# Attention in front of two expert layers: the second batch's v loads issued by GpSimd, raw weights issued two steps sooner, the decoder's VectorE part behind the normalisation

## The chip, the cores and the metric

The kernel runs on one core of one Trainium2 chip. The metric is the device time of one execution in microseconds (us), and the figure that stands for a kernel is the median of its timed runs. A profile is one more execution, recorded by the hardware profiler; its span runs from the first to the last instruction. The engines are called PE (TensorE, matrix products), DVE (VectorE), ACT (ScalarE), POOL (GpSimd) and SP (SyncE, which only issues transfers here).

## The reference, cut to what matters

```python
# q, k, v: (2 batches, 8 heads, 576 rows, 64), float32
scores = scale * np.matmul(q, k.transpose(0, 1, 3, 2))
mask_plain = (rel >= 0) & (rel < 32)                      # heads 0 to 3
mask_dil = (rel >= 0) & (rel < 128) & (rel % 4 == 0)      # heads 4 to 7
scores = np.where(masks, scores, -1e9)
attn = softmax(scores)                                    # with + 1e-9 in the sum
x = np.matmul(attn, v)                                    # then (2 * 576, 512)
...
h = x @ w_in                                              # first layer, 512 -> 2048 -> 512
g = h * np.tanh(softplus(h))
x = g @ w_out
...
for e in range(4):                                        # second layer, 4 experts
    out += p[:, e:e+1] * (np.maximum(x @ w1[e], 0.0) @ w2[e])
```

The weights `w_in` and `w_out` arrive as 64-bit floats, 8 bytes for each value.

## The kernel before

Attention is cut into ten units, `au[0]` to `au[9]`: five chunks of up to 128 rows (`c` = 0 to 4, the last one of 64 rows) in each of two batches. Every unit passes the same stations: its k and q are loaded (`load_k`, `load_q`, four buffers each), transposed by PE, spread by ACT into `kk` and `qq` (`spread`), multiplied (`scores`, one PSUM bank), put through `softmax` (DVE twice, ACT once), transposed again (`probsT` on PE, `probsT_copy` on ACT), multiplied with v (`values`, PSUM bank 4), divided by the row sums (`sums`, `normalise`, both DVE), transposed (`xT`) and split into a high and a low part (`x_hi` on ACT, `x_lo` on DVE) in `xh` and `xl`, which the first layer reads.

A window of keys reaches back 32 rows (or 32 rows of every fourth row), so v is kept in two tiles, `vP` (heads 0 to 3) and `vD` (heads 4 to 7), in which half of the partitions hold a chunk's own rows and the other half those before them. The own half is loaded from memory, as one list of transfers for each range of chunks (`v_loads`; eight transfers for two chunks, six for the last one, ten for chunks 2 to 4). The other half is copied from it by POOL, chunk by chunk (`copy_v(c)`), and `values` of a chunk needs both. One pair of tiles serves both batches: the loads of the second batch overwrite what the first batch has used.

The order on every engine is written out by hand: each engine runs its instructions in the order of the program text, and waits on semaphores where another engine's result is needed. A wait holds up all that stands behind it on that engine. A prologue handles units 0 to 4 as single calls, then `att_step(s)` runs for s = 3 to 7, with unit s at its scores, unit s-1 at its values, unit s-2 at its last transposition and unit s+2 at its first. So `values` of unit 4 is in step 5, of unit 5 in step 6, of unit 6 in step 7, and of units 7, 8 and 9 behind the steps. The copies of step s are those of unit s+1: chunk 4 of the first batch in step 3, chunks 0 to 3 of the second batch in steps 4 to 7.

All transfers are issued by SP. `load(jobs, *large)` deals a list of small v transfers out between large ones: the second batch's v come in three lists, ahead of step 3 with the k and q of unit 8, behind step 4 with two raw weight loads, and behind step 5 with one.

The raw weights are the 64-bit floats, loaded in halves of a unit of 512 KB (`dec_load`, four buffers), and decoded to 32 bits in pieces that lie between the attention's work from step 6 (`DEC0`) on: `dec_dve` (two DVE instructions, the first of which waits for the raw load, lines 151 and 158), then `dec_act` (ACT lines 168 and 175, POOL line 176), which also asks for the next raw load.

Behind the attention come the first layer (`Step1`, lines 570 and 592) and the second (lines 777 and 852), in which PE works without a break.

Of the kernel before, what the change touches and what calls it, by code (L numbers as in the profile page):

```python
# [23 lines left out]
def kernel(  # L24
# [13 lines left out]
    PE, ACT, DVE, POOL, SP = nc.tensor, nc.scalar, nc.vector, nc.gpsimd, nc.sync  # L38
# [70 lines left out]
    def unit_tiles(u):  # L109
        n = slice(1024 * u, 1024 * (u + 1))  # L110
        if u < NUA:
            units[u] = (wxh[:, n], wxl[:, n])
        elif u == NUA:
            units[u] = late[0:2]
        else:
            n = slice(1024 * (u - NUA - 1), 1024 * (u - NUA))
            units[u] = (late[2][:, n], late[3][:, n])
# [4 lines left out]
    def dec_load():  # L122


        if nld[0] >= len(halves) or not free_raws:
            return
        u, part = halves[nld[0]]
        nld[0] += 1
        t = free_raws.pop(0)
        dst = t[:, 1:4097]  # L130
        if part == 0:
            SP.dma_start(out=dst.rearrange("p (c f) -> p c f", c=4),
                         in_=w_in.bitcast(U8)[:, 1024 * u:1024 * (u + 1)].rearrange("(c p) f -> p c f", p=128))
        else:
            SP.dma_start(out=dst, in_=w_out.bitcast(U8)[128 * u:128 * (u + 1), :])
        staged[u, part] = t

    def half_at(n):
        return halves[n] if 0 <= n < len(halves) else None

    def part_cols(part):
        return slice(512 * part, 512 * part + 512)

    def dec_dve():


        n = ndec[0]
        h = half_at(n)
        if h:

            DVE.tensor_scalar(out=kwbuf[n % 3], in0=staged[h].bitcast(U32)[:, 2:1026:2], scalar1=24, scalar2=None,
                              op0=ALU.logical_shift_left)
        h = half_at(n - 1)
        if h:

            kw = kwbuf[(n - 1) % 3]
            t = staged.pop(h)
            DVE.scalar_tensor_tensor(out=kw, in0=t.bitcast(U32)[:, 1:1025:2], scalar=5, in1=kw,
                                     op0=ALU.logical_shift_right, op1=ALU.bitwise_or)
            free_raws.append(t)  # L160

    def dec_act():
        n = ndec[0]
        h = half_at(n)
        if h:

            kw = kwbuf[n % 3]
            ACT.activation(kw.bitcast(F16)[:, 1:1024:2], kw.bitcast(F32), AF.Copy)
        h = half_at(n - 1)
        if h:  # L170
            u, part = h
            if part == 0:
                unit_tiles(u)
            w, (hi, lo) = kwbuf[(n - 1) % 3].bitcast(F32), (t[:, part_cols(part)] for t in units[u])
            ACT.activation(hi, w, AF.Copy)
            POOL.tensor_tensor(out=lo, in0=w, in1=hi.bitcast(F32), op=ALU.subtract)
            dec_load()
        ndec[0] += 1
# [8 lines left out]
    NCH = (S + 127) // 128  # L187
# [61 lines left out]
    def keep():  # L249
        t = bank(7)  # L250
        for n in range(2):
            PE.matmul(t, warm[:, 0:128], warm, start=n == 0, stop=n == 1)
# [6 lines left out]
    def v_loads(b, c0, c1):  # L259

        g0, g1 = 4 * c0, min(4 * c1, S // 32)
        cf = min(c1, S // 128)
        jobs = []
        for j in range(2):
            own = slice(64 * j + 32, 64 * j + 64)
            for p in range(2):
                src = v[b, 2 * p + j:2 * p + j + 1]
                jobs.append((vP[own, p, g0:g1, j, :],
                             bass.AP(src.tensor, src.offset + 32 * g0 * D, [[D, 32], [32 * D, g1 - g0], [1, D]])))
            src = v[b, 4 + j:5 + j]  # L270
            for p in range(2 if cf > c0 else 0):
                jobs.append((vD[own, p, j, c0:cf, :],
                             bass.AP(src.tensor, src.offset + (2 * p * S + 128 * c0) * D,
                                     [[4 * D, 32], [128 * D, cf - c0], [1, 4 * D]])))
            if cf < c1:
                n = (S - 128 * cf) // 4
                jobs.append((vD[64 * j + 32:64 * j + 32 + n, :, j, cf, :],
                             bass.AP(src.tensor, src.offset + 128 * cf * D, [[4 * D, n], [2 * S * D, 2], [1, 4 * D]])))
        return jobs

    def load(jobs, *large):

        large = [w for w in large if w]
        step = -(-len(jobs) // len(large)) if large else len(jobs)
        for i in range(0, max(len(jobs), step), step):
            for o, x in jobs[i:i + step]:
                SP.dma_start(out=o, in_=x)
            if large:
                large.pop(0)()
        for w in large:  # L290
            w()

    def copy_v(c):

        g0, g1 = max(4 * c, 1), min(4 * c + 4, S // 32)
        for j in range(2):
            before, own = slice(64 * j, 64 * j + 32), slice(64 * j + 32, 64 * j + 64)
            POOL.tensor_copy(vP[before, :, g0:g1, j, :], vP[own, :, g0 - 1:g1 - 1, j, :])
            if c:
                POOL.tensor_copy(vD[before, :, j, c, :], vD[own, :, j, c - 1, :])  # L300
# [151 lines left out]
    au = [Unit(b, c) for b in range(B) for c in range(NCH)]  # L452
    NA = len(au)
    u0, u1, u2, u3, u4 = au[0:5]
    for u in (u0, u1, u2):
        u.load_k()
        u.load_q()
    first = v_loads(0, 0, 2)
    load(first[0:6], u3.load_k)
    load(first[6:8], u3.load_q)  # L460

    u0.transposes()
    u4.load_k()
    u4.load_q()
    copy_v(0)
    u0.spread()
    u1.transposes([0])
    u0.scores()
    u1.spread_k(range(2))
    u1.transposes([1])  # L470
    u1.spread_q()
    u0.softmax()
    u2.transposes()
    load(v_loads(0, 2, NCH)[0:8])
    load(v_loads(0, 2, NCH)[8:10], au[5].load_k, au[5].load_q)

    copy_v(1)
    zero_v(2)
# [33 lines left out]
    u0.x_lo()  # L512
    u2.probsT()
    u4.transposes()
    load(v_loads(1, 0, 2), au[8].load_k, au[8].load_q)

    def att_step(s):
        n2, n1, u, p1, p2 = (au[n] for n in (s + 2, s + 1, s, s - 1, s - 2))
        dec = s >= DEC0
        p1.probsT_copy()  # L520
        copy_v(n1.c)
        n1.spread()
        u.scores()
        u.softmax()
        if dec:
            dec_dve()
            keep()
        p1.sums()
        p1.values()
        p2.xT()  # L530
        p1.normalise()
        p2.x_hi()
        if dec:
            dec_act()
        p2.x_lo()
        n2.transposes()
        u.probsT()

        if s == 3:
            au[9].load_k()  # L540
            au[9].load_q()
        elif s == 4:
            load(v_loads(1, 2, 4), dec_load, dec_load)
        elif s == 5:
            load(v_loads(1, 4, NCH), dec_load)
        elif s == 6:
            dec_load()

# [58 lines left out]
    for n in (0, 1):  # L607
        o = 2 * GW * (n + 1)
# [285 lines left out]
    for s in range(3, NA - 2):  # L894
        att_step(s)
    SP.dma_start(out=prob, in_=probs.rearrange("(t p) e -> p t e", p=128))

    u3, u2, u1 = au[NA - 3:]
# [153 lines left out]
```

## Time and profile before

| | us |
|---|---|
| median of 3 timed runs | 649.11 |
| lowest and highest of them | 648.29, 3526.74 |
| the profiled execution's own time | 646.37 |
| its span | 644.5 |
| mean granted clock of PE in it | 0.993 |

The profiled execution took 1.9 us more than its span, and 2.7 us less than the median. Terms read from the span carry over to the median as differences.

### The profile page before, as it was taken

What the parts mean: (1) busy time and instruction counts of PE and PEld (TensorE: products, weight loads), DVE (VectorE), ACT (ScalarE), POOL (GpSimd) and SP (SyncE); (2) the same over time, 40 slices, a digit from 0 to 9 for tenths busy, and PEclk for the clock granted to TensorE, in tenths of its full rate; (3) what the DMA queues carried; (4) which work ended last, traced back from release to release, by engine and by line L of the source; (5) the groups of instructions that cost most, each with busy time, mean ns of one, the idle gap of its engine ahead of it and who ended that gap; (6) DMA issues with size and microseconds to landing.
All of it is one profiled execution on the core that took longest, in us unless ns stands there. A gap on an engine that the chain in (4) does not pass through costs nothing.

```text
span 644.5 us, 10164 instructions
## 1 busy us (share of the span) xinstructions
PE 629.7 (98%) x4156; PEld 561.5 (87%) x4158; DVE 287.8 (45%) x482; ACT 262.0 (41%) x497; POOL 179.1 (28%) x201
## 2 busy tenths in 40 slices
PE   8879999999999999999999999999999999999997
PEld 4757788889999999898989899898899998899986
DVE  5767777632211324454443522534522544523223
ACT  6666877643232344433244322344222334322220
POOL 8743455531200143152134300143300244200000
PEclk9998999999999999999999999999999999999999
DMA  9883576500000221210022300032200023000102
GB/s 187 171 215 110 187 228 208 187 0 1 1 1 1 65 66 66 66 66 3 0 66 99 98 1 1 1 98 84 81 1 0 22 81 95 2 2 14 52 1 81
DMA packets 51358, 43.66 MB, mean 68 GB/s; under 512 B 26352, under 2 KB 44144, under 8 KB 51312
## 3 DMA queue, kind: packets, MB, share of 16 engines
q1 hardware_dynamic: 51312, 43.02, 23.7%
q8 instruction: 32, 0.52, 0.3%
q14 instruction: 14, 0.11, 0.1%
HBM read 40.65 MB, written 2.36 MB: 67 GB/s over the span
## 4 chain that ended last, share of the span: by engine, by line
PE 92%; DMA 3%; ACT 2%; SPq 1%; issue 1%; DVE 1%; POOL 0%; DVEq 0%; POOLq 0%; ACTq 0%
PE bank L852 31%; PE bank L777 26%; PE bank L592 16%; PE bank L570 15%; DMA natq<-in_q_dram 2%; DMA vP<-in_v_dram 1%; SPq L322 1%; PE bank L405 1%; ACT late L619 1%; PE bank L335 1%; PE bank L438 1%; PE bank L417 1%; PE bank L375 1%; PE bank L421 1%; PE bank L383 0%
## 5 line engine op out<-in xcount | busy, mean ns | idle before, releaser
L777 PE MATMUL bank<-xh,late 128*128 128x256 f32 (+1 forms) x512 | 120.1, 295 | 2.6 <-ACT late L789 1.6
L777 PE MATMUL bank<-wxh,late 128*128 128x320 f32 (+1 forms) x384 | 94.0, 294 | 0.0
L777 PEld LDWEIGHTS bank<-xh,late 128*128 128x128 f32 x512 | 88.6, 188 | 5.6 <-ACT late L789 2.2
L852 PE MATMUL bank<-late,gh 128*128 128x512 f32 x288 | 89.3, 391 | 0.0
L570 PE MATMUL bank<-xh,late 128*128 128x320 f32 (+1 forms) x288 | 76.5, 337 | 0.0
L777 PE MATMUL bank<-xl,late 128*128 128x256 f32 (+1 forms) x256 | 75.3, 294 | 0.0
L592 PE MATMUL bank<-gh,late 128*128 128x320 f32 (+1 forms) x288 | 72.6, 337 | 0.0
L731 POOL TENSOR_TENSOR raw<-raw 128x256 f32<-128x256 f32 x16 | 12.2, 763 | 216.2 <-DVE late L620 210.3
L777 PEld LDWEIGHTS bank<-wxh,late 128*128 128x128 f32 x384 | 67.9, 188 | 0.6
L579 DVE TENSOR_TENSOR gl<-scr,gh 128x512 fp32r<-128x512 f32 (+1 forms) x32 | 24.4, 764 | 82.0 <-ACT gh L578 82.0
L852 PEld LDWEIGHTS bank<-late,gh 128*128 128x128 f32 x288 | 52.3, 188 | 9.6
L620 POOL TENSOR_TENSOR late<-raw,late 128x1024 fp32r<-128x1024 f32 x16 | 38.8, 2426 | 73.0 <-ACT late L619 73.0
L575 ACT ACTIVATE scr<-bank 128x320 f32<-128x320 f32 (+1 forms) x48 | 23.5, 490 | 85.7 <-PE bank L570 85.6
L852 PE MATMUL bank<-late,gl 128*128 128x512 f32 x144 | 56.7, 394 | 0.0
L777 PE MATMUL bank<-wxl,late 128*128 128x256 f32 (+1 forms) x192 | 56.6, 295 | 0.1
L570 PEld LDWEIGHTS bank<-xh,late 128*128 128x128 f32 x288 | 50.7, 188 | 4.3
L592 PEld LDWEIGHTS bank<-gh,late 128*128 128x128 f32 x288 | 50.1, 188 | 4.2
L619 ACT ACTIVATE late<-raw 128x512 fp32r<-128x512 f32 (+1 forms) x64 | 48.0, 781 | 12.7 <-PE bank L852 12.7
L852 PE MATMUL bank<-late,late 128*128 128x512 f32 (+1 forms) x219 | 52.8, 388 | 0.0
L777 PEld LDWEIGHTS bank<-xl,late 128*128 128x128 f32 x256 | 48.1, 188 | 1.9
L570 PE MATMUL bank<-xl,late 128*128 128x320 f32 (+1 forms) x144 | 48.6, 337 | 0.0
L592 PE MATMUL bank<-gl,late 128*128 128x320 f32 (+1 forms) x144 | 48.6, 337 | 0.0
(152 smaller groups left out, 1133.5 us busy)
## 6 DMA issues: line engine op xcount, KB each, us to landing
raw<-in_moe_w_dram SPq DMA_DIRECT2D x32, 512.0 KB, 3.5
raw<-in_moe_w_out_dram SPq DMA_DIRECT2D x15, 512.0 KB, 3.6
raw<-in_moe_w_in_dram SPq DMA_DIRECT2D x9, 512.0 KB, 4.1
scr<-in_moe_w_in_dram SPq DMA_DIRECT2D x7, 512.0 KB, 4.3
natk<-in_k_dram SPq DMA_DIRECT2D x8, 256.0 KB, 4.5
natq<-in_q_dram SPq DMA_DIRECT2D x8, 256.0 KB, 4.9
out_dram<-scr SPq DMA_DIRECT2D x8, 256.0 KB, 2.0
vD<-in_v_dram SPq DMA_DIRECT2D x16, 64.0 KB, 3.4
```

Of the source, the lines that this page charges most:

```text
L322: SP.dma_start(out=t[0:self.n], in_=src[self.b, :, rows, :].rearrange("h t d -> t h d"))
L335: PE.transpose(o, nat[0:n, 128 * a:128 * a + 128], ident[0:n, 0:n])
L375: PE.matmul(s[32 * g:32 * g + 32, 128 * p:128 * p + 128], qq[:, p, t:t + 32], kk[:, p, :, t + 96:t + 160], start=False, stop=True, skip_gr ...
L570: PE.matmul(h, a[:, c, :], x[:, c, :], start=c == 0 and k == 0, stop=c == 3 and k == 2)
L575: ACT.activation(self.hc[:, self.w * i:self.w * (i + 1)], h, AF.Mish)
L579: DVE.tensor_tensor(out=self.glo, in0=self.hc, in1=self.ghi.bitcast(F32), op=ALU.subtract)
L592: PE.matmul(yacc[self.grp][d], a[:, 512 + 128 * d:640 + 128 * d], x[:, g], start=u == UORD[self.grp][0] and k == 0, stop=u == UORD[self.gr ...
L619: ACT.activation(hi, src, AF.Copy)
L620: eng.tensor_tensor(out=lo, in0=src, in1=hi.bitcast(F32), op=ALU.subtract)
L731: POOL.tensor_tensor(out=a22, in0=a21, in1=a22, op=ALU.add)
L777: PE.matmul(out, w, x(k), start=first and k == 0 and i == 0, stop=k == 1 and i == 2, skip_group_check=not first)
L852: PE.matmul(acc, x[:, s], a[:, cols], start=self.p == 0 and f == 0 and i == 0, stop=self.p == NP2 - 1 and f == 1 and i == 2, skip_group_ch ...
```

## The change

The v loads of the second batch, three lists of 8, 8 and 6 transfers, are issued by POOL (`load_v`) at the same three places of the text, and no longer by SP. The first raw load moves from behind step 4 to a place ahead of step 3; the second and third stay behind steps 4 and 5 and the fourth behind step 6, now with no v transfers around them in SP's queue. In the prologue the first batch's v transfers of chunks 2 to 4 (`v1`) are issued sooner and between the k and q of units 4 and 5, and unit 5's k and q now stand ahead of the last five and the last three of them. In `att_step`, `dec_dve` stands behind `normalise` and `x_hi` and no longer ahead of `sums`. `load` takes transfers and calls in the order in which they are given.

```diff
--- before.py
+++ after.py
@@ -278,17 +278,16 @@
                              bass.AP(src.tensor, src.offset + 128 * cf * D, [[4 * D, n], [2 * S * D, 2], [1, 4 * D]])))
         return jobs
 
-    def load(jobs, *large):
-
-        large = [w for w in large if w]
-        step = -(-len(jobs) // len(large)) if large else len(jobs)
-        for i in range(0, max(len(jobs), step), step):
-            for o, x in jobs[i:i + step]:
-                SP.dma_start(out=o, in_=x)
-            if large:
-                large.pop(0)()
-        for w in large:
-            w()
+    def load(*jobs):
+        for job in jobs:
+            if callable(job):
+                job()
+            else:
+                SP.dma_start(out=job[0], in_=job[1])
+
+    def load_v(jobs):
+        for o, x in jobs:
+            POOL.dma_start(out=o, in_=x)
 
     def copy_v(c):
 
@@ -455,24 +454,21 @@
     for u in (u0, u1, u2):
         u.load_k()
         u.load_q()
-    first = v_loads(0, 0, 2)
-    load(first[0:6], u3.load_k)
-    load(first[6:8], u3.load_q)
+    v0, v1 = v_loads(0, 0, 2), v_loads(0, 2, NCH)
+    load(*v0[0:6], u3.load_k, *v0[6:8], u3.load_q, v1[0])
 
     u0.transposes()
-    u4.load_k()
-    u4.load_q()
+    load(u4.load_k, v1[1], u4.load_q, *v1[2:5])
     copy_v(0)
     u0.spread()
     u1.transposes([0])
     u0.scores()
     u1.spread_k(range(2))
     u1.transposes([1])
+    load(au[5].load_k, *v1[5:7], au[5].load_q, *v1[7:10])
     u1.spread_q()
     u0.softmax()
     u2.transposes()
-    load(v_loads(0, 2, NCH)[0:8])
-    load(v_loads(0, 2, NCH)[8:10], au[5].load_k, au[5].load_q)
 
     copy_v(1)
     zero_v(2)
@@ -512,7 +508,9 @@
     u0.x_lo()
     u2.probsT()
     u4.transposes()
-    load(v_loads(1, 0, 2), au[8].load_k, au[8].load_q)
+    vl = [v_loads(1, *c) for c in ((0, 2), (2, 4), (4, NCH))]
+    load(au[8].load_k, au[8].load_q, dec_load)
+    load_v(vl[0])
 
     def att_step(s):
         n2, n1, u, p1, p2 = (au[n] for n in (s + 2, s + 1, s, s - 1, s - 2))
@@ -523,7 +521,6 @@
         u.scores()
         u.softmax()
         if dec:
-            dec_dve()
             keep()
         p1.sums()
         p1.values()
@@ -531,6 +528,7 @@
         p1.normalise()
         p2.x_hi()
         if dec:
+            dec_dve()
             dec_act()
         p2.x_lo()
         n2.transposes()
@@ -540,9 +538,11 @@
             au[9].load_k()
             au[9].load_q()
         elif s == 4:
-            load(v_loads(1, 2, 4), dec_load, dec_load)
+            dec_load()
+            load_v(vl[1])
         elif s == 5:
-            load(v_loads(1, 4, NCH), dec_load)
+            dec_load()
+            load_v(vl[2])
         elif s == 6:
             dec_load()
```

## Rows read from the trace of the kernel before

**Rows 1.** Chain that ended last, by engine, of the whole span, from the page.

```profile
PE 92%; DMA 3%; ACT 2%; SPq 1%; issue 1%; DVE 1%; POOL 0%; DVEq 0%; POOLq 0%; ACTq 0%
```

**Rows 2.** Waits of PE behind the attention: waiter, releaser, us, times, longest.

```profile
PE bank L777 <- ACT late L789: 1.6, 3, 0.5
```

**Rows 3.** Stretches: busy us (and instructions) by engine, granted clock, DMA share, GB/s.

```profile
20.00:24.00 4.00, 3.01 (x75) 2.31 (x72) 2.97 (x6) 2.64 (x9) 3.86 (x8) 1.00 0.90 202
...
36.00:40.00 4.00, 3.84 (x62) 2.92 (x63) 1.38 (x2) 2.12 (x4) 1.83 (x4) 1.00 0.80 179
40.00:44.00 4.00, 1.21 (x33) 0.73 (x26) 1.60 (x5) 1.32 (x3) 1.17 (x2) 1.00 1.09 232
44.00:48.00 4.00, 3.37 (x45) 2.60 (x46) 3.93 (x8) 3.24 (x6) 2.33 (x4) 0.68 0.73 241
48.00:52.00 4.00, 4.00 (x53) 3.06 (x57) 2.12 (x5) 2.42 (x8) 3.06 (x5) 0.50 0.64 177
52.00:56.00 4.00, 4.00 (x41) 3.22 (x33) 3.79 (x9) 2.27 (x4) 0.78 (x2) 0.97 0.25 60
```

**Rows 4.** PE in order of time: start, us, line, tiles, count, [idle before].

```profile
21.80 0.62 PE L421 MATMUL bank<-vD,pT 128*32 128x128 f32 x16
...
24.26 0.63 PE L335 MATMUL bank<-ident,natk 128*128 128x128 f32 x4 [1.25 <-ACT xh L446]
25.28 0.63 PE L335 MATMUL bank<-ident,natq 128*128 128x128 f32 x4 [0.40 <-DMA natq<-in_q_dram]
...
31.69 0.50 PE L417 MATMUL bank<-vP,pT 128*32 128x128 f32 x6
...
36.53 0.64 PE L417 MATMUL bank<-vP,pT 128*32 128x128 f32 x16
...
40.81 0.39 PE L252 MATMUL bank<-warm 128*128 128x512 bf16 x1
44.63 0.65 PE L417 MATMUL bank<-vP,pT 128*32 128x128 f32 x16 [3.42 <-POOL vP L298]
...
51.17 1.08 PE L417 MATMUL bank<-vP,pT 128*32 128x128 f32 x16
...
57.48 0.29 PE L417 MATMUL bank<-vP,pT 128*32 128x128 f32 x2
```

**Rows 5.** DVE in order of time.

```profile
42.22 0.43 DVE L151 TENSOR_SCALAR scr<-raw 128x512 uint32<-128x512 uint32 x1 [4.68 <-DMA raw<-in_moe_w_in_dram]
...
43.79 0.69 DVE L429 TENSOR_TENSOR xn<-bank,sm 128x512 f32<-128x512 f32 x1
```

**Rows 6.** POOL in order of time.

```profile
26.64 0.52 POOL L203 MEMSET vD<- 64x512 f32 x1
27.21 0.39 POOL L298 COPY vP<-vP 32x256 f32<-32x256 f32 x1
...
28.55 0.61 POOL L300 COPY vD<-vD 32x512 f32<-32x512 f32 x1
31.09 0.50 POOL L298 COPY vP<-vP 32x384 f32<-32x384 f32 x1 [1.92 <-DMA vP<-in_v_dram]
...
42.81 0.61 POOL L298 COPY vP<-vP 32x512 f32<-32x512 f32 x1 [2.88 <-DMA vP<-in_v_dram]
```

**Rows 7.** SP's issues of v: ns of one, min/median/max; then us to landing.

```profile
L287 SPq DMA_DIRECT2D vP<-in_v_dram x16: 311/447/1658, 13.3 to 43.0; - x16
...
DMA to landing us min/median/max: 2.2/4.0/4.7
```

**Rows 8.** SP in order of time.

```profile
18.09 0.93 SPq L287 DMA_DIRECT2D vD<-in_v_dram x2
19.12 0.38 SPq L322 DMA_DIRECT2D natk<-in_k_dram  x1
...
36.10 1.56 SPq L132 DMA_DIRECT2D raw<-in_moe_w_in_dram  x1
```

**Rows 9.** Issues between 36 and 37 us: KB, us from issue to landing.

```profile
raw<-in_moe_w_in_dram SPq DMA_DIRECT2D x1, 512.0 KB, 6.0
```

## The prediction, made before the change was run

> **What bounds the kernel now.** I read the chain that ended last first: PE carries 92% of it [rows 1]. Then the waits of PE behind the attention: the longest entry is 1.6 us in all, the longest single wait 0.5 us [rows 2]. From there on PE has no gap that this change could fill, so what the change gives is what it moves the end of the attention, some 62 us into the span, and it reaches the total one for one. A measurement of this kernel can tell about 2% (13 us) from no change.
>
> Next the stretches of 4 us [rows 3]. Two stand out. Between 40 and 44 us PE is busy for 1.21 us of 4. Behind that the granted clock is 0.68, 0.50 and 0.97 of full speed (the 0.50 is 1.2 GHz, the lower of the two levels) while PE shows 3.37, 4.00 and 4.00 us of work. The time lost to the clock is 4 x (0.32 + 0.50 + 0.03) = 3.4 us. The smaller gap lies between 20 and 24 us.
>
> Then the engines in order of time, to find what opened the large gap. PE stops at 41.20 (40.81 + 0.39) and takes up `values` of unit 6 at 44.63, 3.42 us later [rows 4]. The trace names a POOL copy as releaser. I don't believe that entry: unit 6 is chunk 1, whose copies were done long before, and the copy that ran then is of a later chunk; in the two steps before, `values` started at 31.69 and 36.53 without such a wait. What did end just then is `normalise` of unit 5 on DVE, from 43.79 to 44.48 [rows 5], which reads the PSUM bank that these `values` write. It was late because DVE stood 4.68 us at line 151, `dec_dve` of step 6, waiting for the first raw load until 42.22 [rows 5]. SP issued that load at 36.10 [rows 8], and it landed 6.0 us after [rows 9]. So the head of the stall is one late transfer, and the fault is that `sums` and `normalise` stand behind it on DVE.
>
> POOL had a wait of its own at that time, 2.88 us until 42.81, for v transfers of chunk 2 [rows 6]. Its copies were then about 7 us ahead of their reader, `values` of unit 7 at 51.17 [rows 4].
>
> **The change, part by part.**
>
> *Raw loads sooner, `dec_dve` behind `normalise`.* One answer for both: the wait at line 151 goes. The first raw load stands behind unit 8's k and q, ahead of step 3, and SP issues it some 5 to 10 us sooner, as 22 v issues of 0.45 us leave its queue [rows 7]. Even with the 6.0 us to landing it is there before step 6 at 36 us. Should it be late, `normalise` no longer stands behind it; `x_lo` of unit s-2 and `dec_act` on ACT do. Taken alone, the gain is the 3.4 us of idle PE and the 3.4 us of slow clock behind it: 6.8 us. What is late next is the question of the POOL part. The new place costs `dec_act` a later start (it follows `values` now), and behind it on ACT stand the next `probsT_copy` and `spread`, which `values` and `scores` need some 4 us later; I cost it at nothing, at most 0.5 us a step for two steps.
>
> *First batch's v and unit 5's k and q in a new order.* PE waited 1.25 and 0.40 us for the transposes of unit 5, at 24.26 and 25.28 [rows 4]; its k was issued at 19.12 [rows 8]. The trace names an ACT operation for the longer wait, but the k transfer of 5.0 us landed then. The new order puts this k and q, 512 KB, ahead of the last v of chunks 2 to 4. At the 202 GB/s of that stretch [rows 3] these v come up to 2.6 us later. The last ones were issued at 18.09 and after [rows 8], and PE used them at 21.80 [rows 4] with little to spare. So the wait of 1.65 us turns into one of 0 to 2 us: worth 0 +- 1.7 us. POOL's copies of chunk 2 wait for some of these v too, which moves POOL by about 0.7 us.
>
> *The v loads on POOL.* This decides. POOL's queue ran without a break to 27.16 (26.64 + 0.52), and then took the copies of chunk 4, 27.21 to 29.16 [rows 6], which `values` of unit 4 needs at 31.69 [rows 4]. The spare time there is 2.5 us. Now eight issues stand ahead of these copies. Behind them stand the copies of chunk 0 (1.1 us), eight issues, the copies of chunk 1 (2.4 us), six issues, and the copies of chunk 2 (2.4 us; one copy is 0.50 to 0.61 us [rows 6]). All of it is in one queue, and the last item frees `values` of unit 7.
>
> No row shows an issue on POOL. From below: the same v transfers took SP 0.31 us at the least and 0.45 in the median [rows 7]; POOL could also hand one over in less, down to nothing. From above: POOL may be held until the data has landed, 4.0 us in the median [rows 7], if an issue there is not let go at once; the longest that SP was held is 1.66 us [rows 7]. I take 0.8 us, between SP's median and SP's longest and nearer to the first: the work is the same in kind, and POOL's own small copies of as many bytes take 0.6 us [rows 6], so I don't expect POOL to be quicker at it than SP.
>
> The Trainium skill, DMA: Bandwidth & Descriptors, "Latency and other measured facts", gives about 1 us to the first byte for transfers issued by GpSimd and about 0.6 us for those of SP. At 1 us for each issue the sum below would end some 4 us later, an estimate from that page; no run here shows it yet.
>
> The sum, with d for one issue. POOL is free at 27.2 + 0.7 = 27.9. The copies of chunk 4 end at 27.9 + 8d + 1.95 = 36.3 for d = 0.8, against 31.69 when PE wants them, and PE is there a little sooner now. So a new stall of about 5 us opens in front of `values` of unit 4, longer than the old one of 3.42, and I let it cost the same drop in clock, 3.4 us. PE's own line from there: from 31.69 to 41.20 was 9.5 us of work, and from 44.63 to 51.17 it was 6.54 with 2.9 lost to the clock (51.17 - 45.4 at half speed), 3.7 at full speed. `values` of unit 7 could start at 36.3 + 9.5 + 3.4 + 3.7 = 52.9. POOL's line: 27.9 + 22d + 1.95 + 1.1 + 2.4 + 2.4 = 35.75 + 22d = 53.35. The later of the two counts: 53.4 against 51.17, 2.2 us late. Before, the slow clock went on to about 52.3, which cost another 0.5 us; that is not paid again. The copies of chunks 3 and 4 follow on POOL at 55.8 and about 59, ahead of their readers (57.48 before [rows 4], plus 1.7). The sum is +1.7 us: the 6.8 us gained are spent, and a little more. From the profiled execution's 646.4 us that is 648.1; from the median of 649.1, which lies 2.7 us higher, it is 650.8, and I say 651.
>
> **The rivals.**
>
> *The issue is cheap* (d up to 0.4). The copies of chunk 4 end by 33, PE waits 1 to 2 us there, too short for what the 1.25 us gap did not do either (clock 1.00 in that stretch [rows 3]), POOL's line ends at 44.6, and `values` of unit 7 starts at about 33 + 9.5 + 3.7 = 46.2: 5 us sooner, with the clock 5.5. That gives 643 to 644. For it speaks that SP does the same in 0.31 to 0.45 us; against it, the copies' 0.6 us.
>
> *The issue is dear: slower than before.* One mechanism: POOL's queue, 22 issues long, holds `values` of unit 7. From d = 1.3 on, POOL's line ends at 64.4, 13 us behind 51.17, with 0.5 given back. That is 662 us, and 22 us more for each further us of d: 677 at d = 2. For it speaks SP's own 1.66 us when its queue was held; against it, that 0.45 us is the median.
>
> *The transfers are the bound, whoever issues them.* Between 40 and 44 us the DMA share is 1.09 [rows 3], and the raw load took 6.0 us to land in company of v [rows 9]. Now up to three more raw loads, 1.5 MB, stand on SP's side while POOL's v come; at 232 to 241 GB/s [rows 3] they take 6.5 us. If v get half of the engines' time meanwhile, the first list lands some 3 us late, and the copies of chunk 0 and all behind them on POOL move with it: 654. The Trainium skill, DMA: Bandwidth & Descriptors, "Issuing engines are not separate DMA queues", speaks for this case: transfers of all issuing engines run on the same 16 DMA engines, and another issuer saves only the time of issuing.
>
> *The change doesn't do what it says.* If the first raw load still lands after step 6 has begun, the stall at 41 us stays, shortened; with the move of `dec_dve` it would hold ACT only. I see no way to that, as its buffer is free from the start.
>
> **How the numbers follow.** The forecast's case, d from 0.5 to 1.1, runs from 645 (stall too short for the clock) to 657 and gets 0.55. Cheap, 641 to 645: 0.20. Transfers the bound, 652 to 657: 0.07. Dear gets 0.18, of which 0.04 lies between 657 and 662 and 0.14 above. That leaves 0.02 of the cheap case below 636 for gains that I don't see, and 0.84 within 2%. The range is 642 to 663: 0.08 lies below it and 0.12 above.
>
> **What would show it.** Right: no wait of DVE at line 151 in step 6; issues on POOL of 0.6 to 1.1 us each from about 28 us; an idle PE of 4 to 6 us ahead of line 417 near 31 to 36 us, with a lower clock behind it; the waits of line 417 on POOL's copies; PE without waits behind 66 us. The step most likely to be wrong is d, a number that no row of before shows; next is whether the new stall costs the clock.

## Result, and the profile after

| | before | after |
|---|---|---|
| median, us (7 runs each, side by side) | 648.29 | 653.49 |
| the profiled execution, us | 646.37 | 651.67 |
| its span, us | 644.5 | 649.9 |
| mean granted clock of PE | 0.993 | 0.997 |

The ratio of after to before is 1.0103, with a 95% interval of 1.0066 to 1.0141: slower by 1.0%, less than the 2% that was to count as a difference, and more than the 0.3% forecast. One execution of before took 3526.74 us and is left out of the ratio.

DVE in order of time, after (start, us, line, tiles, [idle before]), answers to [rows 5]:

```profile
44.09 0.42 DVE L151 TENSOR_SCALAR scr<-raw 128x512 uint32<-128x512 uint32 x1
...
53.80 1.09 DVE L158 SCALAR_TENSOR_TENSOR scr<-raw,scr 128x512 uint32<-128x512 uint32 x1
```

The 4.68 us of idle ahead of line 151 are gone. What the change was to remove, it removed. Now PE in order of time, after, against [rows 4] (line 416 is `values`, 417 before):

```profile
22.16 0.64 PE L416 MATMUL bank<-vP,pT 128*32 128x128 f32 x16 [0.53 <-POOL vP L297]
...
24.27 0.66 PE L420 MATMUL bank<-vD,pT 128*32 128x128 f32 x16 [1.47 <-issue]
...
34.82 0.63 PE L416 MATMUL bank<-vP,pT 128*32 128x128 f32 x8 [2.46 <-POOL vP L297]
...
41.33 0.65 PE L416 MATMUL bank<-vP,pT 128*32 128x128 f32 x16
...
47.62 0.64 PE L416 MATMUL bank<-vP,pT 128*32 128x128 f32 x16 [1.61 <-POOL vP L297]
...
53.09 0.64 PE L416 MATMUL bank<-vP,pT 128*32 128x128 f32 x16 [1.12 <-POOL vP L297]
...
57.98 0.50 PE L570 MATMUL bank<-xh,wxl 128*128 128x512 f32 x1 [2.64 <-POOL wxl L176]
...
68.92 0.50 PE L592 MATMUL bank<-gh,wxh 128*128 128x512 f32 x1 [0.34 <-ACT gh L578]
```

Before, `values` of units 4 to 7 began at 31.69, 36.53, 44.63 and 51.17; here it is 34.82, 41.33, 47.62 and 53.09, so 3.1, 4.8, 3.0 and 1.9 us later. One stall of 3.42 us has become waits of 2.46, 1.61, 1.12 and 2.64 us, each with a POOL instruction as releaser; in each the named instruction, or the copy that these `values` read, ends 0.05 us before PE starts. The first product at line 592, which I use as the mark of the end of the attention, comes at 68.92 against 64.47 before: 4.45 us. The last PE instruction starts 4.5 us later; the other 0.9 us of the longer span lie behind it, up to the last landing of the output.

POOL in order of time, after, against [rows 6] (line 290 issues v, 297 and 299 copy it):

```profile
28.75 1.31 POOL L290 DMA_DIRECT2D vP<-in_v_dram  x2
30.04 1.07 POOL L290 DMA_DIRECT2D vD<-in_v_dram  x2
...
33.37 0.39 POOL L297 COPY vP<-vP 32x256 f32<-32x256 f32 x1
...
34.71 0.61 POOL L299 COPY vD<-vD 32x512 f32<-32x512 f32 x1
37.74 0.50 POOL L297 COPY vP<-vP 32x384 f32<-32x384 f32 x1 [2.42 <-DMA vP<-in_v_dram]
40.66 0.50 POOL L297 COPY vP<-vP 32x384 f32<-32x384 f32 x1 [2.43 <-DMA vP<-in_v_dram]
41.21 1.16 POOL L290 DMA_DIRECT2D vP<-in_v_dram  x2
...
52.98 0.61 POOL L299 COPY vD<-vD 32x512 f32<-32x512 f32 x1
...
54.29 1.06 POOL L299 COPY vD<-vD 32x512 f32<-32x512 f32 x1
...
55.96 0.61 POOL L299 COPY vD<-vD 32x512 f32<-32x512 f32 x1
56.65 1.28 POOL L176 TENSOR_TENSOR wxl<-scr,wxh 128x512 fp32r<-128x512 f32 x1
```

Two issues together take 1.06 to 1.31 us, one takes 0.50 to 0.65; all 22 take 12.3 us, 0.56 in the mean. The eight of the first list stand ahead of the copies of chunk 4 (33.37 to 35.32), for which unit 4 waits. From 41.21 on POOL runs without a gap until 60, and what it does last is what PE waits for: the decoder's subtraction at line 176 ends at 57.93, behind the copies of chunk 3, and PE's line 570 starts at 57.98. Before, POOL was idle and waited for ACT at this subtraction:

```profile
48.83 1.28 POOL L176 TENSOR_TENSOR wxl<-scr,wxh 128x512 fp32r<-128x512 f32 x1 [2.41 <-ACT wxh L175]
```

After, ACT had written the same input by 51.77, 4.9 us before POOL came to it:

```profile
51.17 0.60 ACT L175 ACTIVATE wxh<-scr 128x512 fp32r<-128x512 f32 x1
```

SP in order of time, after, against [rows 8]:

```profile
27.35 1.04 SPq L132 DMA_DIRECT2D raw<-in_moe_w_in_dram  x1
...
29.97 1.51 SPq L132 DMA_DIRECT2D raw<-in_moe_w_in_dram  x1
...
31.57 0.84 SPq L135 DMA_DIRECT2D raw<-in_moe_w_out_dram  x1
...
32.51 0.64 SPq L132 DMA_DIRECT2D scr<-in_moe_w_in_dram  x1
```

The transfers issued between 31 and 35 us, after (KB, median us from issue to landing), against [rows 9]:

```profile
raw<-in_moe_w_in_dram SPq DMA_DIRECT2D x1, 512.0 KB, 11.5
raw<-in_moe_w_out_dram SPq DMA_DIRECT2D x1, 512.0 KB, 11.1
scr<-in_moe_w_in_dram SPq DMA_DIRECT2D x1, 512.0 KB, 12.5
vD<-in_v_dram POOLq DMA_DIRECT2D x3, 64.0 KB, 8.6
vP<-in_v_dram POOLq DMA_DIRECT2D x2, 64.0 KB, 8.8
```

With no v in its queue SP runs far ahead of the steps: all four raw loads, 2 MB, have left by 33.2 us, while POOL issues the first list of v. These v take 8.6 to 8.8 us to land in the median (the first list as a whole 7.5 to 8.9), where v took 4.0 in the median before [rows 7], and the copies of chunk 0 wait 2.42 and 2.43 us for them.

Stretches of 4 us, after, columns as in [rows 3]:

```profile
32.00:36.00 4.00, 1.54 (x40) 0.88 (x28) 2.58 (x6) 2.02 (x4) 3.22 (x7) 0.96 1.20 158
36.00:40.00 4.00, 4.00 (x33) 3.42 (x29) 1.35 (x3) 0.97 (x2) 0.50 (x1) 0.62 1.08 243
...
44.00:48.00 4.00, 2.39 (x54) 1.52 (x53) 3.02 (x7) 3.40 (x6) 3.92 (x8) 1.00 0.30 90
...
52.00:56.00 4.00, 2.26 (x38) 1.44 (x38) 3.90 (x6) 3.11 (x9) 3.86 (x7) 1.00 0.67 140
56.00:60.00 4.00, 2.02 (x9) 1.67 (x10) 2.76 (x6) 0.64 (x2) 3.81 (x6) 1.00 0.42 134
```

Behind unit 4's gap the granted clock falls to 0.62 for one stretch: 4 x (0.04 + 0.38) = 1.7 us, half of the 3.4 before. The four stretches behind 32 us in which PE is busy for 1.54 to 2.39 us are where the time is.

### The profile page after: what moved, and what is told of

It is laid out like the page before. It is cut to its first block, busy times and chain, and to the rows that moved or that the text cites. A ratio compares the mean times of both kernels' runs of the same rounds, so it can differ in the third digit from the quotient of the medians.

```text
span 649.9 us, 10166 instructions
## 1 busy us (share of the span) xinstructions
PE 629.4 (97%) x4156; PEld 560.4 (86%) x4158; DVE 289.3 (45%) x482; ACT 262.2 (40%) x497; POOL 192.4 (30%) x223
## 3 DMA queue, kind: packets, MB, share of 16 engines
q0 software_dynamic: 704, 1.18, 0.8%
## 4 chain that ended last, share of the span: by engine, by line
PE 89%; POOL 3%; DMA 2%; ACT 2%; SPq 1%; issue 1%; DVE 1%; DVEq 0%; POOLq 0%; ACTq 0%
PE bank L852 30%; PE bank L777 26%; PE bank L592 16%; PE bank L570 15%; DMA vP<-in_v_dram 2%; POOL vP L290 1%; SPq L321 1%; POOL vP L297 1%; ACT late L619 1%; POOL vD L299 1%; SPq L286 1%; POOL vD L290 1%; DMA vD<-in_v_dram 1%; DVE gl L814 0%; PE bank L420 0%
```

## Experiments

The theory: the raw loads and `dec_dve` bring a gain, as was forecast, and the v loads on POOL more than take it away, by POOL's time for the issues, by their place ahead of chunk 4's copies, and by the raw loads that then collide with v. The rivals: POOL's issues are cheap and the collision alone costs; the collision is harmless and POOL's queue alone costs; the prologue costs. Each ratio below is to the kernel before on the same chip. "Lost" is PE's idle time plus the time lost to the clock from 20 us to the mark, summed over the stretches of 4 us of the profiled execution (busy share and granted clock of each, worked out as above).

| kernel | ratio, 95% interval | lost, us | mark, us |
|---|---|---|---|
| before | 1 | 9.0 | 64.47 |
| after | 1.0103 [1.0066, 1.0141] | 12.0 | 68.92 |
| dve_only | 0.9969 [0.9951, 0.9987] | 7.4 | 63.72 |
| raw_only | 0.9978 [0.9958, 0.9998] | 8.4 | 64.44 |
| both | 0.9965 [0.9945, 0.9985] | 6.7 | 62.92 |
| prologue_only | 0.9990 [0.9969, 1.0012] | 8.3 | 64.69 |
| v_on_sp | 0.9954 [0.9930, 0.9978] | 5.4 | 61.94 |
| raw_held | 1.0051 [1.0031, 1.0072] | 10.0 | 66.49 |
| one_raw | 1.0066 [1.0036, 1.0096] | 11.3 | 68.06 |
| copies_first | 1.0068 [1.0045, 1.0092] | 11.6 | 68.17 |
| pool_fill | 1.0016 [0.9995, 1.0037] | 7.2 | 63.60 |
| second_raw_mid | 0.9954 [0.9937, 0.9972] | 5.1 | 61.86 |
| second_raw_first | 0.9969 [0.9952, 0.9985] | 4.5 | 61.18 |
| sub_first | 0.9960 [0.9943, 0.9976] | 5.7 | 62.36 |

**dve_only**: before, with the move of `dec_dve` alone.

```diff
         if dec:
-            dec_dve()
             keep()
...
         if dec:
+            dec_dve()
             dec_act()
```

> The kernel before, with dec_dve of a step moved behind normalise and x_hi, and nothing else. The first raw load still lands near 42 us. Theory A (POOL's queue, 22 issues of 0.56 us each and the copies behind them, is what costs the time) and theory B (the raw loads, issued sooner, share the DMA engines with v, whose landing takes 5.9 us instead of 3.5 to 4) both expect little: normalise of unit 5 is on time, but dec_act on ACT still waits for line 151, and the next probsT_copy stands behind it, so values of unit 6 start at about 43.9 instead of 44.6. Ratio to before 0.997 to 1.000.

PE of this kernel, `values` of unit 6:

```profile
43.86 0.64 PE L417 MATMUL bank<-vP,pT 128*32 128x128 f32 x16 [2.43 <-POOL vP L298]
```

The wait is 1 us shorter, not gone: `normalise` is free, but `dec_act` on ACT now stands behind the late raw load, and `probsT_copy` behind it ends only at 43.76, just before PE starts. (The POOL copy that the trace names belongs to a later chunk.) 0.3% faster.

**raw_only**: before, with the first raw load ahead of step 3 and one fewer behind step 4; v stays on SP.

```diff
     load(v_loads(1, 0, 2), au[8].load_k, au[8].load_q)
+    dec_load()
...
-            load(v_loads(1, 2, 4), dec_load, dec_load)
+            load(v_loads(1, 2, 4), dec_load)
```

> The kernel before, with the first raw load issued ahead of step 3 and the later ones one earlier, and nothing else; v stays on SP. Theory A: the stall at 41 us and the slow clock behind it go, 5 to 7 us, ratio 0.989 to 0.993. Theory B: the raw load ahead of v in SP's queue makes v land 2 us or more later, POOL's copies of chunks 1 and 2 move with it, and values of unit 6 or 7 wait for them; ratio 0.995 to 1.003.

PE of this kernel, `values` of unit 7:

```profile
48.80 1.08 PE L417 MATMUL bank<-vP,pT 128*32 128x128 f32 x16 [3.33 <-ACT pT L410]
```

The stall moves one unit on, to the second raw load. The ratio lies in theory B's range, but not for its reason, which was that v would land late behind the first raw load. **both** joins the two edits.

> The kernel before with two of the four edits: raw loads sooner and dec_dve behind normalise. v stays on SP and the prologue keeps its old order. Each edit alone left a wait of 2.4 or 3.3 us at unit 6 or 7 that the other one is meant to take away. If the prologue's new order is what cost the version with v on SP its early waits (2.5 us at unit 2 and a lower clock behind them), this is 2 to 4 us faster than that one: ratio to before 0.988 to 0.992. If the prologue's order is neutral, as the prediction had it (0 +- 1.7 us), it is like that one: 0.994 to 0.997.

PE and DVE of this kernel about unit 7, one line of each:

```profile
46.27 0.43 DVE L151 TENSOR_SCALAR scr<-raw 128x512 uint32<-128x512 uint32 x1 [2.22 <-DMA raw<-in_moe_w_in_dram]
48.56 0.64 PE L417 MATMUL bank<-vP,pT 128*32 128x128 f32 x16 [3.14 <-issue]
```

The two gains don't add up: the second raw load, issued at 40.70 behind eight v on SP, lands 5.5 us later and holds step 7 for 3.14 us.

**prologue_only**: before, with the change's three prologue lines (the first three edits of `load` calls in the diff above).

> The kernel before with the prologue's new order of the first batch's v and unit 5's k and q, and nothing else. The prediction: a wait of 1.65 us turns into one of 0 to 2 us, worth 0 +- 1.7 us, ratio 0.997 to 1.003. The rival, that the order alone costs 2 to 4 us (unit 2's values wait for v, and the clock may fall behind that): 1.003 to 1.006.

No difference, as forecast (0 ± 1.7 us). Its trace bears out the prediction's reading of the old stall: the wait of unit 6's `values`, 2.90 us at 44.81, is put down here to `normalise` on DVE and not to a POOL copy. It shows one more thing that matters below: POOL waits 3.90 us until 22.97 for a v transfer of the first batch, where it waited 0.18 until 19.85 before, and comes to the copies of chunk 4 at 30.33, against 27.21 [rows 6].

**v_on_sp**: after, with the second batch's v back on SP.

```diff
-    load(au[8].load_k, au[8].load_q, dec_load)
-    load_v(vl[0])
+    load(*vl[0][0:4], au[8].load_k, *vl[0][4:8], au[8].load_q, dec_load)
...
-            dec_load()
-            load_v(vl[1])
+            load(*vl[1], dec_load)
...
-            dec_load()
-            load_v(vl[2])
+            load(*vl[2], dec_load)
```

> The changed kernel, with the second batch's v issued by SP again, dealt out around the loads of unit 8 as before; raw loads sooner, the prologue's order and the place of dec_dve stay as changed. Theory A: all of the loss is on POOL, so this is faster than before by the stall at 41 us, ratio 0.988 to 0.993. Theory B: raw loads among the v still delay v, a wait of values on POOL's copies stays, ratio 0.997 to 1.005.

PE of this kernel; these are all of its waits over 0.4 us between 18 and 70 us:

```profile
22.87 0.64 PE L416 MATMUL bank<-vP,pT 128*32 128x128 f32 x16 [0.91 <-POOL vP L297]
...
25.13 1.08 PE L420 MATMUL bank<-vD,pT 128*32 128x128 f32 x16 [1.62 <-issue]
...
49.14 0.65 PE L416 MATMUL bank<-vP,pT 128*32 128x128 f32 x16 [0.62 <-issue]
```

This is the experiment that decides the main question. All that differs from after is who issues 22 transfers and where they stand among SP's others, and all four waits of after on POOL from 34 us on are gone. 0.9954 against 1.0103: the move of v to POOL costs 1.5%, some 9.7 us, and the rest of the change is worth a gain of 0.5%. The ratio lies between the ranges of the two theories: the loss is all in the move of v, but the gain that is left is smaller than theory A had it.

**raw_held** asks how much of this is the collision: after, with the four raw loads held back behind v (each waits for a small POOL memset of its buffer, which now stands behind the first and second list).

```diff
-    for t in free_raws:
-        POOL.memset(t[:, 4096:4104].bitcast(U32), 0)
...
-    load(au[8].load_k, au[8].load_q, dec_load)
     load_v(vl[0])
+    held = list(free_raws)
+    POOL.memset(held[0][:, 4096:4104].bitcast(U32), 0)
+    load(au[8].load_k, au[8].load_q)
...
+            load(au[9].load_k, au[9].load_q, dec_load)
...
-            dec_load()
             load_v(vl[1])
+            for t in held[1:4]:
+                POOL.memset(t[:, 4096:4104].bitcast(U32), 0)
+            dec_load()
```

> The changed kernel, with the v on POOL, but the raw loads held back by their buffers' small memsets: the first is let go when POOL has issued the first list of v (33 us), the others when it has issued the second. Theory A: the wait of unit 4's values (2.5 us) and the later ones stay, as the POOL queue is unchanged; ratio 1.008 to 1.011, as for the change. Theory B: the first list of v lands in 3.5 to 4 us instead of 5.9, POOL's two waits of 2.4 us for it go, all behind them on POOL is 3 to 5 us sooner, and the waits at units 6 and 7 and at line 570 go; only the wait of unit 4 stays, ratio 1.000 to 1.005.

Landings of POOL's v in this kernel, over the whole span (KB, median us):

```profile
vP<-in_v_dram POOLq DMA_DIRECT2D x8, 64.0 KB, 2.5
vD<-in_v_dram POOLq DMA_DIRECT2D x8, 64.0 KB, 2.2
```

PE of this kernel:

```profile
36.38 0.63 PE L414 MATMUL bank<-vP,pT 128*32 128x128 f32 x8 [2.73 <-POOL vP L295]
...
53.70 0.64 PE L414 MATMUL bank<-vP,pT 128*32 128x128 f32 x16 [1.69 <-POOL vD L297]
```

POOL and ACT of this kernel, the last copy of chunk 2 and unit 7's `probsT_copy`:

```profile
49.89 0.61 POOL L297 COPY vD<-vD 32x512 f32<-32x512 f32 x1
...
53.03 0.58 ACT L407 ACTIVATE pT<-bank 128x512 f32<-128x512 f32 x1
```

Out of the raw loads' way v lands in 2.2 to 2.5 us in the median (the first list in 2.1 to 3.6), and POOL waits for none of the second batch's. That takes 0.5% off after (1.0103 to 1.0051; the intervals overlap a little). The wait for POOL's copies at unit 4 remains, with POOL's own queue behind it, and those at unit 6 and line 570 are gone, as theory B had it. Unit 7 still waits, but not for POOL: the copy that the trace names is of chunk 3, and the copies of chunk 2, which unit 7 reads, ended at 50.50. What ended at 53.61, just before PE starts, is `probsT_copy` on ACT. It stands behind `dec_act`, which waited for DVE's lines 151 and 158.

**one_raw**: after, with the first raw load let go and the other three held back.

```diff
-    for t in free_raws:
-        POOL.memset(t[:, 4096:4104].bitcast(U32), 0)
+    POOL.memset(free_raws[0][:, 4096:4104].bitcast(U32), 0)
+    held = free_raws[1:4]
...
-            dec_load()
             load_v(vl[1])
+            for t in held:
+                POOL.memset(t[:, 4096:4104].bitcast(U32), 0)
+            dec_load()
```

> The changed kernel with only the first raw load let go at once; the other three are held back (by their buffers' small memsets on POOL) until POOL has issued the second v list. In the changed kernel all four went out between 27.4 and 33.2 us, since no v stood in SP's queue to hold them up, and landed 9 to 12.5 us after issue, the first v list 7.7 to 8.8 us. Theory: the three that follow, not the one that was moved, are what the v collide with: the first v list lands in 4 to 5 us, ratio to before 1.003 to 1.007. Rival: the first one is enough to delay v, ratio 1.008 to 1.011.

1.0066, not clearly apart from raw_held. The first list landed in 4.7 to 6.7 us, slower than I expected: one raw load beside v already does part of the harm. (In after the first raw load landed in 7.3 us, and the other three in 11.1 to 12.5.)

**copies_first**: raw_held, with the first list of v behind the copies of chunk 4.

```diff
         copy_v(n1.c)
+        if s == 3:
+            load_v(vl[0])
+            POOL.memset(held[0][:, 4096:4104].bitcast(U32), 0)
```

> The version with v on POOL and raw loads held back, with the first list of v issued behind the copies of chunk 4 instead of ahead of them, and the first raw load let go behind that list. If standing ahead of the copies is the cost, the wait of unit 4 (2.7 us, and the lower clock behind it) goes, the copies of chunk 0 come 1 to 2 us later in time for unit 5, and it is 4 to 6 us faster than that version: ratio to before 0.996 to 0.999. If the sum of POOL's 22 issues is the cost, the wait only moves from unit 4 to unit 5 or 7: ratio 1.003 to 1.006.

PE of this kernel:

```profile
45.46 0.64 PE L414 MATMUL bank<-vP,pT 128*32 128x128 f32 x16 [1.02 <-POOL vP L295]
...
50.78 0.65 PE L414 MATMUL bank<-vP,pT 128*32 128x128 f32 x16 [1.11 <-POOL vP L295]
...
55.67 0.69 PE L572 MATMUL bank<-xh,wxl 128*128 128x512 f32 x1 [2.63 <-POOL wxl L176]
```

Unit 4 waits no more, and nothing is gained: the wait turns up at units 6 and 7 and at line 572. At unit 6 POOL is not alone, as the raw load that is let go later keeps DVE's line 151 waiting for 1.18 us and ACT's `probsT_copy` behind it ends at 45.36, 0.11 us after the copy. The part of my theory about the place of the list falls. It is the sum of POOL's queue that is late: the one other order that was tried makes later readers wait.

**pool_fill** adds to "both" (v on SP) only time on POOL: memsets of an unused tile, 8, 8 and 6 of them, where after has its issues. This is extra work; the output doesn't depend on it.

```diff
+    fill = ap1.tile([64, 504], F32, name="fill")
...
     dec_load()
+    pool_fill(8)
...
             load(v_loads(1, 2, 4), dec_load)
+            pool_fill(8)
...
             load(v_loads(1, 4, NCH), dec_load)
+            pool_fill(6)
```

> The version with raw loads sooner and dec_dve behind normalise, v still on SP, and on POOL 8, 8 and 6 memsets of 64x504 (about 0.52 us each, 11.4 us in all) at the three places where the change issues v. They stand for the time of the 22 issues on POOL alone, with no transfer behind them. Theory A: POOL's queue makes unit 4 wait about 2 us and puts the copies behind the readers: 3 to 6 us slower than the version without them, ratio to before 0.996 to 1.002. If the issue time by itself is hidden and only the transfers matter: as the version without them, 0.988 to 0.992.

POOL of this kernel, the first eight:

```profile
27.62 4.50 POOL L296 MEMSET fill<- 64x504 f32 x8
```

PE of this kernel:

```profile
33.63 0.63 PE L422 MATMUL bank<-vP,pT 128*32 128x128 f32 x8 [2.22 <-POOL vP L303]
...
50.84 0.65 PE L422 MATMUL bank<-vP,pT 128*32 128x128 f32 x16 [1.58 <-POOL vP L303]
```

The same 0.56 us each, with no transfer in it, opens the same wait at unit 4 (2.46 in after). The wait at unit 7 is again one for ACT and not for POOL: chunk 2's copies ended at 48.29, `probsT_copy` at 50.74. The filling costs 0.5% against "both" by the ratios, whose intervals lie apart (medians 647.61 and 643.70); the two profiled executions, of 645.61 and 645.82 us, don't show it. So POOL's time for the issues costs some 3 us, and the collision of the raw loads, less surely, another 3.

**second_raw_mid, second_raw_first, sub_first** look for a better version, from "both": the second raw load between the halves of the second v list, ahead of it, and, with the first of these, step 7's copies behind the decoder's subtraction.

```diff
-            load(v_loads(1, 2, 4), dec_load)
+            jobs = v_loads(1, 2, 4)
+            load(jobs[0:4], dec_load)
+            load(jobs[4:8])
```
```diff
-            load(v_loads(1, 2, 4), dec_load)
+            dec_load()
+            load(v_loads(1, 2, 4))
```
```diff
-        copy_v(n1.c)
+        if s < 7:
+            copy_v(n1.c)
...
             dec_act()
+        if s == 7:
+            copy_v(n1.c)
```

> The version with two edits (raw loads sooner, dec_dve behind normalise, v on SP) with the second raw load issued between the two halves of the second v list instead of behind it. Theory: its wait of 3.1 us at unit 7 is line 151 waiting for the second raw load (issued at 40.7, landed at 46.2, DVE idle 2.2 us), which ACT's dec_act and the next probsT_copy stand behind. Issued 3 to 4 us sooner it lands before 43, the wait goes and so does the lower clock behind it: 3 to 6 us faster than that version, ratio to before 0.988 to 0.992. Rival: the raw load delays the second half of v by 2 us or more, POOL's copies of chunk 2 end behind 46, and unit 7 waits for them: 0.994 to 0.997, as before.

> As the version with the second raw load between the halves of the second v list, but with that load ahead of the whole list. All eight v transfers now stand behind it in SP's queue. If v have 2 us to spare there, the same 0.988 to 0.992; if they don't, unit 7 waits on POOL's copies of chunk 2 and this is 1 to 4 us slower than the other one, 0.992 to 0.997.

> The version with the second raw load between the halves of the second v list, with step 7's copies of chunk 3 behind the decoder's POOL subtraction (line 176) of that step instead of ahead of it. In that version PE waited 1.5 us at the first layer's third product for that subtraction, which stood behind 2.4 us of copies that unit 8 reads only some 7 us later. Theory (what stands ahead in POOL's queue is what costs): the wait goes, 1 to 2 us faster, ratio to before 0.992 to 0.995. Rival: the subtraction waits for ACT anyway, or unit 8 now waits for its copies; ratio as without the edit, 0.994 to 0.997.

PE of second_raw_mid:

```profile
47.30 0.64 PE L417 MATMUL bank<-vP,pT 128*32 128x128 f32 x16 [1.61 <-POOL vD L300]
...
50.92 0.50 PE L573 MATMUL bank<-xh,wxl 128*128 128x512 f32 x1 [1.49 <-POOL wxl L176]
```

A stretch of sub_first, columns as in [rows 3]:

```profile
24.00:28.00 4.00, 3.10 (x17) 2.10 (x19) 1.96 (x4) 1.24 (x3) 3.82 (x9) 0.74 1.03 229
```

All three are 0.3 to 0.5% faster than before and can't be told from one another or from "both"; none reached the gain that was hoped for (0.988 to 0.992, and 0.992 to 0.995 for sub_first). In second_raw_mid the wait at unit 7 is halved, and a new one stands at line 573, for POOL's subtraction behind copies; sub_first removes that one as expected, but has a new wait of 1.11 us at 58.38 for ACT's part of a `softmax`, and its profile shows a lower clock at 24 to 28 us. The wait at unit 7 ends in all three 0.1 us behind ACT's `probsT_copy`. second_raw_mid and v_on_sp, both at 0.9954, are the best of the study: 0.5% below before and 1.5% below after.

## Why the prediction was right or wrong

The sign and the rough size held: 651 was forecast, 653.49 came, with the forecast's own mechanism, a stall exchanged for POOL's queue. Forecast was +1.7 us; the medians differ by 5.2, the spans by 5.4. That it came so near is in part luck, as two of its errors cancelled. By its steps:

- **The wait at line 151 goes.** Right; dve_only and raw_only show that either edit alone leaves a wait, and "both" that the next raw load takes the place of the first. The forecast's 6.8 us for the two was too much: they bring 0.35%, 2 us. After's raw loads are all early only because SP has no v to issue.
- **The new place of `dec_dve`, at nothing to 0.5 us a step.** Too small where nothing else is late: with v on SP, unit 7 waits 0.62 us (v_on_sp) and 0.84 (sub_first) for `probsT_copy` behind `dec_act`, and in raw_held, where line 158 took 1.09 us beside POOL's copies, 1.69. In after POOL's copies are later still and cover it.
- **The prologue's order, 0 ± 1.7 us.** Right for PE (0.9990). For POOL I took 0.7 us; in after it came to the end of the work ahead of unit 4's copies at 28.75 and not at 27.21 (1.5 us), in prologue_only at 30.33 (3.1). Over all profiles this point lies at 27.21 to 27.88 with the old order (eight kernels) and at 28.75 to 30.78 with the new one (six).
- **d = 0.8 us for one issue.** Too high: 0.56, inside the bounds. Over 22 issues this put 0.24 x 22 = 5.3 us too much on POOL's line.
- **POOL's line without waits.** Wrong. I summed issues and copies and left out that the copies of chunk 0 wait for what has just been issued: 2.42 + 2.43 = 4.85 us. The rival "the transfers are the bound" named this with 3 us and 0.07; it was no rival but a term of the sum. With the start 0.85 us late, 53.35 + 0.85 - 5.3 + 4.85 = 53.75, and the copies of chunk 2 ended at 53.59. `values` of unit 7, forecast for 53.4, began at 53.09: two errors of 5 us cancelled there, by luck.
- **A new stall at unit 4 with a drop of the clock.** Right in kind, 2.46 us and not 5, since d is smaller; the drop cost 1.7 us, not 3.4.
- **The copies of chunks 3 and 4 are ahead of their readers.** This is the step that failed, and it is most of the 3.7 us by which the forecast missed (the spans' 5.4 less 1.7); another 0.9 us is the later landing of the output, which no run explains. The copies were in time for `values`, but behind the copies of chunk 3 stands the decoder's subtraction at line 176, which I had not put on POOL's line, and line 570 waits 2.64 us for it. The lateness of 1.9 us at unit 7 plus these 2.64 is about the 4.45 us at the mark.
- **What stood on SP.** I said that the raw loads would leave sooner once 22 issues were out of SP's queue, and gave no price to it beyond the rival: the v issues had been what kept the second to fourth raw load back.

The Trainium skill, DMA: Bandwidth & Descriptors, "Issuing engines are not separate DMA queues", which stood for that rival, is borne out: the first list of v, issued by POOL, took 7.5 to 8.9 us beside SP's raw loads (after), and 2.1 to 3.6 without them (raw_held).

What stays open: of the 1.5% that v on POOL costs, pool_fill gives POOL's time 0.5% and raw_held the collision 0.5%. The rest, some 3 us, fits the new prologue: it makes POOL late (30.15 for the first issue in raw_held, against 27.62 for the first memset in pool_fill, which has the old prologue; after itself was at 28.75), and this has spare time to vanish in when v is on SP, and none when the issues stand on POOL. The marks of the two differ by 2.9 us, the starts by 2.5. But no run put POOL's issues behind the old prologue, so this is read from traces and not shown. Nor does "lost" cover the whole of the marks: the differences of the two agree to about 1.5 us.

## What to carry to other kernels

Put an issue on an engine only after writing down its whole queue from there to the next reader, with the instructions of other helpers on it and with the landing of each transfer that a later entry waits for: a queue that was 2.5 us ahead of its reader can't take in 4.5 us. An engine's queue of issues is also a brake for the transfers behind them; take the small ones out, and ask what will now leave early and land on top of what. Two edits that remove the same stall are not worth their sum, since the next late transfer in line sets what the pair brings.

## What the hardware showed that I had not expected

- An issue on POOL holds POOL for 0.50 to 0.65 us, longer than SP's median of 0.45 [rows 7], and was not lengthened by the raw loads in flight: the first eight took 4.62 us in after and 4.61 in raw_held, which holds those loads back.
- With the raw loads out of the way, 64 KB issued by POOL land in 2.2 to 2.5 us in the median (raw_held). The Trainium skill, DMA: Bandwidth & Descriptors, "Anatomy of one DMA — SWDGE (gpsimd) path", gives a fixed 2.0 us plus the bytes at 436 GB/s, an estimate of 2.15 us from that page; raw_held's medians agree, and after's first list, with 7.5 to 8.9, shows what company adds.
- DVE's line 158 and a POOL copy slow each other when they meet: 1.09 and 1.06 us at 53.80 and 54.29 in after, against 0.69 for line 158 at 50.39, when POOL only issued, and 0.61 for the same copy at 55.96.
- A PE gap of like size did not always have the same clock behind it: before kept 1.00 from 24 to 28 us over waits of 1.25 and 0.40 us at unit 5's transposes [rows 4], and sub_first, with 1.09 and 0.53 us at the same place, fell to 0.74 there and 0.83 in the next stretch. After kept 1.00 behind the 2.64 us at line 570. No run here says what decides.
